# The last step of the last group: another order of its products, half sums in PSUM, an order written out, and two sums on GpSimd

## The chip, the cores and the metric

One Trainium2 chip, one core. The metric is the device time in microseconds of the whole program; it is one launch. TensorE (PE) multiplies, VectorE (DVE) and ScalarE (ACT) read and write PSUM and SBUF, GpSimd (POOL) works on SBUF only, SyncE (SP) issues the DMAs.

## The reference

Three stages follow each other, all in float32: an attention through 32 packed queries per head, a dense layer pair with SiLU, and a layer of 8 experts that are all computed for each token. Only the last stage matters here:

```python
P = ...                      # [2304, 8], normalised by rows and columns 8 times
out = zeros((2304, 512))
for e in range(8):
    h = maximum(x @ w1[e], 0)        # [2304, 1024]
    out += P[:, e:e+1] * (h @ w2[e]) # [2304, 512]
```

## The kernel before

The tokens of the last stage are three groups; groups 1 and 2 have 1024 tokens each. A group takes 16 steps, one for each expert `e` and half `fh` of its 1024 hidden columns; group 2, steps 32 to 47, ends the program. Matrices are held as a high part (ScalarE's cast) and a low part (VectorE's difference, `split`, L144 and L145), and a product is three matmuls, high by high, low by high, high by low.

In groups 1 and 2 each of the two products of a step is done by Strassen-Winograd's scheme with seven products of half-size blocks in place of eight; they are numbered 1 to 7. `up` computes h (transposed) into four blocks `hb`; `h_forms` makes from them the operands of the seven down products, each a high and a low tile out of pools with three buffers (`form`). `down7(s, p)` computes product `p` of step `s` for two halves `d` of the output rows: 6 matmuls into one PSUM bank of a pool `p3` of four, and the result is added to `M[p]`, one of seven sums that live through the group. Either the bank is first seeded with `M[p]` by ScalarE (L1125) and ScalarE copies the result back (L1137), or VectorE adds the bank to `M[p]` (L1141).

At the last step of a group the seven sums are combined: output blocks are M1 + M2, and M3, M5 and M4 after M6 (which has M1 added) and M7 have been added to them. In the kernel before, the last step of the last group (`LORD`) goes 1, 3, 5, 6, 7, 2, 4; M2 + M1 is one 1024-wide VectorE operation (L1143), M5 + M6 and M3 + M5 (L1145, L1146) stand behind product 6, M5 + M7 and M7 + M6 (L1149, L1151) behind product 7, and product 4 is folded with M7 by VectorE, one half at a time (L1133). `flush` sends the blocks out from the SP queue: 512 KB whole (L1107) or 256 KB by halves (L1109).

`moe_step(s)` makes the order of the text: per position `n` it draws the next form, computes `up` of step `s` and `down7` of step `s - 1`, and fetches weights three products ahead (`w2_get`, `w2_block`). At `s = 48` there is no `up` any more, only the down products of step 47. The parts of the program before step 17 of this stage run under `tc.manual_schedule` with PE, DVE and ACT: on these engines the instructions keep the order of the text. From step 17 on, the scheduler of the tile framework orders the instructions of each engine itself, by the text's order and by when it takes their inputs to be ready. Instructions inside a manual region keep their order among each other; those outside may go between them.

Of the kernel before, what the change touches and what calls it, by code (L numbers as in the profile page):

```python
# [9 lines left out]
F32 = mybir.dt.float32  # L10
# [14 lines left out]
NB = 512  # L25
# [79 lines left out]
def fused_kernel(  # L105
# [647 lines left out]
    G0 = 2 * NE  # L753
    ORD = [1, 2, 6, 7, 5, 3, 4]
    DORD = [1, 3, 7, 5, 6, 2, 4]
    LORD = [1, 3, 5, 6, 7, 2, 4]

    def dord(s):
        return LORD if s == NS - 1 else DORD

# [309 lines left out]
    def h_forms(s):  # L1070

        b11, b12, b21, b22 = (hb[s, f, t] for f in range(2) for t in range(2))

        def form(p, x):
            hi = st["hi"].tile([128, 2, NB], F32R, tag="hi", name=f"hi{s}_{p}")
            lo = st["lo"].tile([128, 2, NB], F32R, tag="lo", name=f"lo{s}_{p}")
            split(hi, lo, x)
            hf[s, p] = hi, lo

        form(1, b11)  # L1080
        yield
        form(3, b22)
        yield
        dve.tensor_tensor(b11, b12, b11, op=ALU.subtract)
        dve.tensor_tensor(b12, b22, b12, op=ALU.subtract)
        if dord(s) is DORD:
            form(7, b12)
            yield
        form(5, b11)
        yield  # L1090
        dve.tensor_tensor(b22, b22, b11, op=ALU.subtract)
        form(6, b22)
        yield
        if dord(s) is LORD:
            form(7, b12)
            yield
        form(2, b21)
        yield
        dve.tensor_tensor(b21, b21, b22, op=ALU.subtract)
        form(4, b21)  # L1100
        yield

    def flush(t, g, dh, th, d=None):
# [4 lines left out]
        else:  # L1108
            nc.sync.dma_start(o[:, d], t[:, d])  # L1109

    def down7(s, p):

        g, e, fh = steps[s]
        first, last = (e, fh) == (0, 0), (e, fh) == (NE - 1, 1)
        if first:
            M[p] = unit([128, 2, NB], F32, f"M{g}{p}")
        (hi, lo), w = hf.pop((s, p)), w2f.pop((s, p))
        for d in ((1, 0) if p == DORD[0] else (0, 1)):
            ps = p3.tile([128, 512], F32, tag="y", name=f"d{s}{p}{d}")
            m = M[p][:, d]  # L1120
            early = last and p == 2 and dord(s) is LORD
            fold = last and p in (6, 2, 4) and not early
            seed = not first and (fold or early or d == 0)
            if seed:
                act.copy(out=ps, in_=m)  # L1125
            n = 0
            for c in range(2):
                for l, r in ((0, hi), (0, lo), (1, hi)):
                    pe.matmul(ps, w[:, l, c, 128 * d:128 * d + 128], r[:, c],  # L1129
                              start=(n == 0 and not seed), stop=(n == 5), skip_group_check=seed)  # L1130
                    n += 1
            if fold:
                dve.tensor_tensor(m, ps, M[{6: 1, 2: 1, 4: 7}[p]][:, d], op=ALU.add)  # L1133
                if p != 6:
                    flush(M[p], g, p // 4, 0, d)
            elif seed or first:
                act.copy(out=m, in_=ps)  # L1137
                if early:
                    flush(M[p], g, 0, 0, d)
            else:  # L1140
                dve.tensor_tensor(m, ps, m, op=ALU.add)  # L1141
        if last and p == 3 and dord(s) is LORD:
            dve.tensor_tensor(M[2], M[2], M[1], op=ALU.add)  # L1143
        if last and p == 6:
            dve.tensor_tensor(M[5], M[5], M[6], op=ALU.add)  # L1145
            dve.tensor_tensor(M[3], M[3], M[5], op=ALU.add)  # L1146
            flush(M[3], g, 0, 1)
        if last and p == (7 if dord(s) is LORD else 6):
            dve.tensor_tensor(M[5], M[7], M[5], op=ALU.add)  # L1149
            flush(M[5], g, 1, 1)  # L1150
            dve.tensor_tensor(M[7], M[7], M[6], op=ALU.add)  # L1151

    X, Y, Z, cp = {}, {}, {}, {}

# [225 lines left out]
        cvn.drain()  # L1380


    def moe_step(s):
        swap = s + 1 < NS and steps[s + 1][0] != steps[s][0]
        hform = h_forms(s - 1) if s > G0 else iter(())
        next(hform, None)
        for n, p in enumerate(ORD):
            if s < NS:
                for i in range(2):
                    up(s, i, p)  # L1390
                if swap:
                    nc.sync.dma_start(x_tile(2, p).bitcast(F32), xfd[p])
                q = 7 * s + n + AHEAD
                if q < 7 * NS:
                    w1_get(q // 7, ORD[q % 7])
                q += 3
                if q < 7 * NS and ORD[q % 7] in (1, 2, 4):
                    w1_block(q // 7, ORD[q % 7])
            if s > G0:
                next(hform, None)  # L1400
                down7(s - 1, dord(s - 1)[n])
            if s == G0 and n == 0:
                load_w2(G0, 0, "r1")
                load_w2(G0, 1, "r1")
            q = 7 * (s - 1) + n + AHEAD
            if G0 <= q // 7 < 2 * G0:
                next(forms)
            elif 2 * G0 <= q // 7 < NS:
                w2_get(q // 7, dord(q // 7)[q % 7])
            q += 3  # L1410
            if 2 * G0 <= q // 7 < NS and dord(q // 7)[q % 7] in (1, 2, 4):
                w2_block(q // 7, dord(q // 7)[q % 7])
            if G0 < s < 2 * G0 - 1 and n == 3:
                next(xg2[0], None)
                next(xg2[0], None)
        if s == 2 * G0 - 2:
            for _ in xg2[0]:
                pass
        if s < NS and s % 2 == 0:
            load_pb(steps[s][0], steps[s][1] + 1)  # L1420

    with tc.manual_schedule(engines={mybir.EngineType.PE, mybir.EngineType.DVE, mybir.EngineType.Activation}):
        sk = sinkhorn()
        next(sk)
        for g in (1, 2):
            for k in range(4):
                tc.keep_in_program_order(nc.sync.dma_start(
                    x2d[k, :, TOK[g]:TOK[g] + 2 * NB],
                    x2[2 - g][k][:, TOK[g] % SB:TOK[g] % SB + 2 * NB]))
        for s_ in (a2a_st, x2a_st, x2b_st, gt_st, hp_st, pt_st, pg_st):  # L1430
            s_.close()
        for name, n in (("xf", 7), ("cp", 5), ("xr", 2), ("pb", 2)):
            open_(name, n, side="left", keep=True)
        open_("acc", 2 * LATE)
        st["u0"], u0_st = pool("pu", 2, space=PSUM, side="left", reuse_waits="tile")

        def chain(*gens):
            for g in gens:
                yield from g

        xg = x_forms(1, x_keep, (4, 4))
        comb = combine()
        for s in range(G0 + 1):
            for j in range(2):
                g, n, h, m = (w2s, s, w1s, s + 2) if j else (w1s, s + 1, w2s, s)
                if s < G0:
                    up0(s, j)
                    sum0(s, j)
                    adv(g, n, 2)
                    adv(g, n, 3)  # L1450
                    relu0(s, j)
                    if 2 * s + j >= 13:
                        next(xg, None)
                if s > 0:
                    down0(s - 1, j)
                if s < G0:
                    adv(g, n, 4)
                    adv(h, m, 1)
                    if s > 0:
                        next(sk, None)  # L1460
                    if s > 2 * LATE + 2:
                        next(comb, None)
                    if 2 * s + j >= 13:
                        next(xg, None)
                    if (s, j) == (G0 - 1, 0):
                        for _ in xg:
                            pass
            if s == G0 - 2:
                for p in ORD[:2]:
                    w1_block(G0, p, "S")  # L1470
            if s == G0 - 3:
                load_pb(1, 0)
            if s == G0 - 1:
                for p in ORD[:AHEAD]:
                    w1_get(G0, p)
        for name in ("acc", "r2", "gh", "xx", "po"):
            closers[name].close()
        u0_st.close()
        st["m"], s_ = pool("pm", 2, space=PSUM, side="left", reuse_waits="tile"); ctx.enter_context(s_)
        for name, n in (("hb", 6), ("hi", 3), ("lo", 3), ("rb", 2)):  # L1480
            open_(name, n, keep=True)
        forms = chain(*(w2_forms(s) for s in range(G0, 2 * G0)))
        xg2 = [x_forms(2, x_store, (1, 2))]
        moe_step(G0)
    for s in range(G0 + 1, NS + 1):
        moe_step(s)

# [51 lines left out]
```

## Time and profile before

| | us |
|---|---|
| median of 3 runs | 1782.55 (1781.41 to 1782.70) |
| the profiled execution | 1782.22 |
| its span, first to last instruction | 1780.5 |

The profile is of one execution. Times in its views are us from the span's start; "idle before" is the time in which the engine had nothing to do just before the first instruction of the row, with what ended it. PEld is TensorE's load of weights, which overlaps its matmuls. The granted clock of TensorE is given as a share of 2.4 GHz. TensorE is busy in 99% of the span, VectorE in 82%, ScalarE in 61%; the last step takes about the last 24 us.

### The profile page before, as it was taken

How to read it: one execution, taken by the hardware profiler on the slowest of the kernel's cores; microseconds unless marked ns; L12 is line 12 of the kernel's file. 1: busy time of each engine (PE TensorE's matmuls, PEld its weight loads, DVE VectorE, ACT ScalarE, POOL GpSimd, SP SyncE). 2: the span in 40 equal slices, each digit the busy share in tenths (PEclk: the TensorE clock that was granted, in tenths of full speed). 3: DMA queues.
4: the chain of work that ended last, by engine and by line, in shares of the span. 5: the costliest groups of instructions: out<-in, count | busy, mean ns of one | idle time of the engine just before them, and what ended most of it. 6: DMA issues, size and time to landing. Idle time of an engine off the chain costs nothing.

```text
span 1780.5 us, 24855 instructions
## 1 busy us (share of the span) xinstructions
PE 1765.2 (99%) x9324; PEld 1495.3 (84%) x9324; DVE 1453.2 (82%) x1950; ACT 1084.5 (61%) x1728; POOL 1.0 (0%) x8
## 2 busy tenths in 40 slices
PE   7999999999999999999999999999999999999998
PEld 5899999988888888888888888888888888888887
DVE  7968796758996989999889999887777777777778
ACT  6866776656664666666666666656555555555555
POOL 0000000000000000000000000000000000000000
PEclk9999999999999999999999999999999999999999
DMA  9326676965664755456545556855555444545442
GB/s 350 143 96 213 241 263 247 335 224 180 213 233 156 256 186 183 162 201 209 169 171 177 172 188 202 317 203 170 157 170 165 155 156 146 172 155 172 148 130 95
DMA packets 141496, 341.72 MB, mean 192 GB/s; under 512 B 11952, under 2 KB 49472, under 8 KB 140480
## 3 DMA queue, kind: packets, MB, share of 16 engines
q1 hardware_dynamic: 141376, 340.14, 56.2%
q8 instruction: 73, 1.20, 0.3%
q14 instruction: 47, 0.39, 0.1%
HBM read 256.66 MB, written 83.44 MB: 191 GB/s over the span
## 4 chain that ended last, share of the span: by engine, by line
PE 95%; DVE 3%; ACT 1%; issue 0%; DMA 0%; DVEq 0%; SPq 0%; ACTq 0%
PE d L1129 34%; PE X L1177 20%; PE Z L1177 10%; PE g2w L689 8%; PE g L600 5%; PE d L1036 5%; PE Y L1177 5%; PE u L1004 3%; PE g L654 3%; PE u L1007 2%; PE u L193 1%; PE s L193 0%; DMA kq<-in_kT_dram 0%; PE lg L1211 0%; DVE nmx L270 0%
## 5 line engine op out<-in xcount | busy, mean ns | idle before, releaser
L145 DVE TENSOR_TENSOR lo<-hb,hi 128x1024 fp32r<-128x1024 f32 x224 | 273.7, 1222 | 33.0 <-ACT hi L144 32.0
L1129 PE MATMUL d<-hi,w2f 128*128 128x512 f32 x896 | 294.2, 389 | 0.0
L1177 PE MATMUL X<-xf,w1l 128*128 128x512 f32 x1152 | 276.9, 389 | 0.0
L144 ACT CAST hi<-hb 128x1024 fp32r<-128x1024 f32 x224 | 235.3, 1051 | 66.8 <-PE d L1129 61.6
L1177 PEld LDWEIGHTS X<-xf,w1l 128*128 128x128 f32 x1152 | 216.2, 188 | 44.9
L1137 ACT COPY M<-d 128x512 f32<-128x512 f32 x234 | 137.2, 588 | 141.5 <-PE d L1129 140.6
L1141 DVE TENSOR_TENSOR M<-d,M 128x512 f32<-128x512 f32 x204 | 140.4, 688 | 100.2 <-PE d L1129 100.2
L1129 PEld LDWEIGHTS d<-hi,w2f 128*128 128x128 f32 x896 | 168.2, 188 | 35.1
L1129 PE MATMUL d<-lo,w2f 128*128 128x512 f32 x448 | 174.3, 389 | 0.0
L1129 PE MATMUL d<-hi,w2l 128*128 128x512 f32 x512 | 167.8, 389 | 0.0
L689 PE MATMUL g2w<-ring,woh 128*128 128x384 f32 x576 | 147.6, 337 | 0.0
L1125 ACT COPY d<-M 128x512 f32<-128x512 f32 x216 | 127.1, 589 | 22.1 <-DVE M L1141 20.4
L1129 PE MATMUL d<-hi,w2g 128*128 128x512 f32 x384 | 125.7, 389 | 0.0
L1129 PEld LDWEIGHTS d<-hi,w2l 128*128 128x128 f32 x512 | 96.1, 188 | 20.2 <-ACT d L1125 0.4
L689 PEld LDWEIGHTS g2w<-ring,woh 128*128 128x128 f32 x576 | 102.9, 188 | 8.6 <-issue 7.5
L1184 ACT COPY cp<-X 128x512 f32<-128x512 f32 x128 | 74.3, 581 | 47.2 <-PE X L1177 47.0
L1129 PE MATMUL d<-lo,w2l 128*128 128x512 f32 x256 | 99.6, 389 | 0.0
L1129 PEld LDWEIGHTS d<-lo,w2f 128*128 128x128 f32 x448 | 84.1, 188 | 17.4
L1177 PE MATMUL Y<-xf,w1f 128*128 128x512 f32 x384 | 97.4, 389 | 0.0
L689 PE MATMUL g2w<-ring,wol 128*128 128x384 f32 x288 | 96.3, 334 | 0.0
L144 ACT CAST w1f<-rb 128x512 fp32r<-128x512 f32 x96 | 59.8, 624 | 57.2 <-PE d L1129 43.4
L1177 PE MATMUL Z<-xf,w1f 128*128 128x512 f32 x384 | 92.2, 389 | 0.0
(220 smaller groups left out, 3428.7 us busy)
## 6 DMA issues: line engine op xcount, KB each, us to landing
r<-in_moe_w_dram SPq DMA_DIRECT2D x128, 512.0 KB, 4.1
w1l<-w1d SPq DMA_DIRECT2D x128, 512.0 KB, 4.0
w1d<-po SPq DMA_DIRECT2D x64, 512.0 KB, 4.4
w2d<-w2f SPq DMA_DIRECT2D x64, 512.0 KB, 4.2
w2l<-w2d SPq DMA_DIRECT2D x64, 512.0 KB, 3.5
rb<-in_moe_w_dram SPq DMA_DIRECT2D x96, 256.0 KB, 2.6
sb<-in_moe_w_dram SPq DMA_DIRECT2D x48, 256.0 KB, 2.7
pb<-pd SPq DMA_DIRECT2D x16, 512.0 KB, 5.2
```

The lines of the kernel that those rows point to most:

```text
L144: act.copy(out=hi, in_=raw)
L145: eng.tensor_tensor(out=lo, in0=raw, in1=hi.bitcast(F32), op=ALU.subtract)
L600: pe.matmul(ps, lhs[:, fs], rhs, start=(n == 0), stop=(n == 5))
L654: pe.matmul(ps[:, :HS], lhs, rhs, start=(n == 0), stop=(n == 3 * nf - 1))
L689: pe.matmul(ps[:, :TW], lhs[:, f % 2, ds], ring[f // 2][:, 2 * (f % 2) + rhs, q], start=(n == 0 and not on), stop=(n == 11), skip_group_ch ...
L1036: pe.matmul(ps, h[:, l, f % 2, 128 * tt:128 * tt + 128], w[:, f % 2], start=(fh == 0 and n == 0), stop=(fh == 1 and n == 11))
L1125: act.copy(out=ps, in_=m)
L1129: pe.matmul(ps, w[:, l, c, 128 * d:128 * d + 128], r[:, c], start=(n == 0 and not seed), stop=(n == 5), skip_group_check=seed)
L1137: act.copy(out=m, in_=ps)
L1141: dve.tensor_tensor(m, ps, m, op=ALU.add)
L1177: pe.matmul(ps, w[:, l, c, 128 * i:128 * i + 128], x[:, r, c], start=(n == 0 and p in (1, 7)), stop=(n == 5), skip_group_check=p in (2, 6, ...
L1184: act.copy(out=t, in_=ps)
```

## The change

The last step of the last group goes through its products as 1, 3, 5, 6, 2, 7, 4. Form 2 is made before form 7, and both are drawn before product 6; form 4 is drawn before product 2. From position 2 on (form 6 and product 5) PE, DVE and ACT run in the order of the text. After the first half of products 5, 6, 2 and 7, both banks of the next product are allocated and, where they are seeded, written (`start7`). Product 7 is seeded in both halves and evicted by ScalarE; M6 (with M1 in it) is added to M7 by halves right after product 6's halves, so that product 7's banks start from M7 + M6. M2 + M1 and M3 + M5 go to GpSimd. M3 + M6 stands ahead of product 7, M5 + M7 behind it. The last step of group 1 keeps its operations.

```diff
-    LORD = [1, 3, 5, 6, 7, 2, 4]
+    LORD = [1, 3, 5, 6, 2, 7, 4]
...
         form(6, b22)
         yield
+        form(2, b21)
+        yield
         if dord(s) is LORD:
             form(7, b12)
             yield
-        form(2, b21)
-        yield
         dve.tensor_tensor(b21, b21, b22, op=ALU.subtract)
         form(4, b21)
         yield
...
+    def start7(s, p, d):
+        first, last = steps[s][1:] == (0, 0), steps[s][1:] == (NE - 1, 1)
+        end = last and dord(s) is LORD
+        if first and p not in M:
+            M[p] = unit([128, 2, NB], F32, f"M{steps[s][0]}{p}")
+        ps = p3.tile([128, 512], F32, tag="y", name=f"d{s}{p}{d}")
+        seed = not first and (d == 0 or (last and p in (6, 2, 4)) or (end and p == 7))
+        if seed:
+            act.copy(out=ps, in_=M[p][:, d])
+        open7[p, d] = ps, seed
...
+        def total(a, b, d=slice(0, 2), eng=dve):
+            eng.tensor_tensor(M[a][:, d], M[a][:, d], M[b][:, d], op=ALU.add)
+        if end and p == 7:
+            total(3, 6)
+            flush(M[3], g, 0, 1)
+        for n, d in enumerate((1, 0) if p == DORD[0] else (0, 1)):
+            if (p, d) not in open7:
+                start7(s, p, d)
+            ps, seed = open7.pop((p, d))
             m = M[p][:, d]
...
-            if fold:
+            if last and (p in (6, 4) or (p == 2 and not end)):
                 dve.tensor_tensor(m, ps, M[{6: 1, 2: 1, 4: 7}[p]][:, d], op=ALU.add)
                 if p != 6:
                     flush(M[p], g, p // 4, 0, d)
+                elif end:
+                    total(7, 6, d)
             elif seed or first:
                 act.copy(out=m, in_=ps)
-                if early:
+                if end and p == 2:
                     flush(M[p], g, 0, 0, d)
             else:
                 dve.tensor_tensor(m, ps, m, op=ALU.add)
-        if last and p == 3 and dord(s) is LORD:
-            dve.tensor_tensor(M[2], M[2], M[1], op=ALU.add)
...
+            if end and n == 0 and p in LORD[2:6]:
+                for x in range(2):
+                    start7(s, LORD[LORD.index(p) + 1], x)
+        if end and p == 3:
+            total(2, 1, eng=nc.gpsimd)
+        if end and p == 5:
+            total(3, 5, eng=nc.gpsimd)
+        if end and p == 7:
+            total(5, 7)
+            flush(M[5], g, 1, 1)
...
+            if s == NS and n == 2:
+                tail.enter_context(tc.manual_schedule(engines=FIXED))
...
                 next(hform, None)
+                if s == NS and n == 3:
+                    next(hform, None)
                 down7(s - 1, dord(s - 1)[n])
```

## Rows read from the trace of the kernel before

**Rows 1.** Page: busy us of each engine, share of the span, instructions.
```profile
PE 1765.2 (99%) x9324; PEld 1495.3 (84%) x9324; DVE 1453.2 (82%) x1950; ACT 1084.5 (61%) x1728; POOL 1.0 (0%) x8
```

**Rows 2.** Chain that ended last, from 1735 us: start, us, what.
```profile
1750.93 2.72 PE Z L1177 x12
1753.65 11.14 PE d L1129 x48
...
1764.81 1.06 ACT hi L144
...
1774.63 1.24 DVE M L1151
```

**Rows 3.** Timeline, PE and PEld, last step: start, us, engine line op [idle before].
```profile
1758.92 0.39 PE L1129 MATMUL d<-hi,w2l 128*128 128x512 f32 x1
...
1761.74 0.19 PEld L1129 LDWEIGHTS d<-hi,w2l 128*128 128x128 f32 x1 [0.36 <-ACT d L1125]
...
1773.51 0.19 PEld L1129 LDWEIGHTS d<-lo,w2g 128*128 128x128 f32 x1 [0.55 <-DVE lo L145]
...
1775.68 0.39 PE L1129 MATMUL d<-hi,w2g 128*128 128x512 f32 x1
```

**Rows 4.** Timeline, VectorE, last step.
```profile
1760.94 1.22 DVE L145 TENSOR_TENSOR lo<-hb,hi 128x1024 fp32r<-128x1024 f32 x1
1762.08 0.68 DVE L1141 TENSOR_TENSOR M<-d,M 128x512 f32<-128x512 f32 x1
1762.68 0.68 DVE L145 TENSOR_TENSOR w2g<-sb,w2g 128x512 fp32r<-128x512 f32 x1
1763.28 1.22 DVE L145 TENSOR_TENSOR lo<-hb,hi 128x1024 fp32r<-128x1024 f32 x1
1764.81 0.69 DVE L1141 TENSOR_TENSOR M<-d,M 128x512 f32<-128x512 f32 x1 [0.31 <-PE d L1129]
1765.90 1.22 DVE L145 TENSOR_TENSOR lo<-hb,hi 128x1024 fp32r<-128x1024 f32 x1 [0.40 <-ACT hi L144]
...
1768.24 1.22 DVE L1099 TENSOR_TENSOR hb<-hb,hb 128x1024 f32<-128x1024 f32 x1
...
1773.38 1.22 DVE L1149 TENSOR_TENSOR M<-M,M 128x1024 f32<-128x1024 f32 x1
1774.63 1.23 DVE L1151 TENSOR_TENSOR M<-M,M 128x1024 f32<-128x1024 f32 x1
1775.99 1.29 DVE L1133 TENSOR_TENSOR M<-d,M 128x512 f32<-128x512 f32 x2
```

**Rows 5.** Timeline, ScalarE, last step.
```profile
1759.66 1.05 ACT L144 CAST hi<-hb 128x1024 fp32r<-128x1024 f32 x1
1760.61 0.58 ACT L1137 COPY M<-d 128x512 f32<-128x512 f32 x1
1761.09 0.60 ACT L1125 COPY d<-M 128x512 f32<-128x512 f32 x1
1761.84 1.05 ACT L144 CAST hi<-hb 128x1024 fp32r<-128x1024 f32 x1 [0.15 <-PE d L1129]
```

**Rows 6.** SP queue's timeline, and one window: us, engines' busy time, clock, DMA share, GB/s.
```profile
1774.62 0.38 SPq L1107 DMA_DIRECT2D out_dram<-M  x1
1776.71 0.93 SPq L1109 DMA_DIRECT2D out_dram<-M  x2
...
1774.00:1775.00 1.00, 1.00 (x6) 0.79 (x5) 0.97 (x2) 0.00 (x0) 0.00 (x0) 1.00 1.05 391
```

**Rows 7.** GpSimd's groups by line: shapes, count | busy us, mean ns | idle before.
```profile
masks.py:199 POOL TENSOR_SCALAR_AFFINE_SELECT ident<-ident 128x128 f32<-128x128 f32 x1 | 0.3, 292 | 0.0
L153 POOL MEMSET ones<- 128x128 f32 x1 | 0.2, 205 | 0.0
```

**Rows 8.** Windows at the end and the start; clock is third from the end.
```profile
1776.07:1780.50 4.43, 0.00 (x1) 0.00 (x0) 1.21 (x2) 0.00 (x0) 0.00 (x0) 1.00 0.59 219
2.00:4.00 2.00, 0.00 (x0) 0.00 (x0) 0.41 (x1) 0.01 (x1) 0.00 (x0) 1.00 0.92 349
...
5.14 1.18 PE L193 MATMUL s<-kq,pTs 64*32 64x288 f32 x8 [5.14 <-DMA kq<-in_kT_dram]
```

More of the change, by code (lines that the diff above doesn't have):

```diff
@@ L1109, in flush @@
             nc.sync.dma_start(o[:, d], t[:, d])
+    open7 = {}
+    def start7(s, p, d):
[8 more added lines that the diff above has]
+        open7[p, d] = ps, seed
     def down7(s, p):
@@ L1114, in down7 @@
         first, last = (e, fh) == (0, 0), (e, fh) == (NE - 1, 1)
+        end = last and dord(s) is LORD
         if first:
-            M[p] = unit([128, 2, NB], F32, f"M{g}{p}")
+            M.pop(p, None)
         (hi, lo), w = hf.pop((s, p)), w2f.pop((s, p))
-        for d in ((1, 0) if p == DORD[0] else (0, 1)):
-            ps = p3.tile([128, 512], F32, tag="y", name=f"d{s}{p}{d}")
-            m = M[p][:, d]
[L1121 to L1126, printed above, removed]
+        def total(a, b, d=slice(0, 2), eng=dve):
[7 more added lines that the diff above has]
+            ps, seed = open7.pop((p, d))
+            m = M[p][:, d]
+            k = 0
             for c in range(2):
@@ L1129, in down7 @@
                     pe.matmul(ps, w[:, l, c, 128 * d:128 * d + 128], r[:, c],
-                              start=(n == 0 and not seed), stop=(n == 5), skip_group_check=seed)
-                    n += 1
-            if fold:
+                              start=(k == 0 and not seed), stop=(k == 5), skip_group_check=seed)
+                    k += 1
+            if last and (p in (6, 4) or (p == 2 and not end)):
                 dve.tensor_tensor(m, ps, M[{6: 1, 2: 1, 4: 7}[p]][:, d], op=ALU.add)
@@ L1141, in down7 @@
                 dve.tensor_tensor(m, ps, m, op=ALU.add)
-        if last and p == 3 and dord(s) is LORD:
-            dve.tensor_tensor(M[2], M[2], M[1], op=ALU.add)
-        if last and p == 6:
-            dve.tensor_tensor(M[5], M[5], M[6], op=ALU.add)
-            dve.tensor_tensor(M[3], M[3], M[5], op=ALU.add)
+            if end and n == 0 and p in LORD[2:6]:
[8 more added lines that the diff above has]
+            flush(M[5], g, 1, 1)
+        if last and not end and p == 6:
+            total(5, 6)
+            total(3, 5)
             flush(M[3], g, 0, 1)
-        if last and p == (7 if dord(s) is LORD else 6):
-            dve.tensor_tensor(M[5], M[7], M[5], op=ALU.add)
+            total(5, 7)
             flush(M[5], g, 1, 1)
-            dve.tensor_tensor(M[7], M[7], M[6], op=ALU.add)
+            total(7, 6)
     X, Y, Z, cp = {}, {}, {}, {}
@@ L1380, in fused_kernel @@
         cvn.drain()
+    FIXED = {mybir.EngineType.PE, mybir.EngineType.DVE, mybir.EngineType.Activation}
+    tail = ExitStack()
     def moe_step(s):
@@ L1420, in moe_step @@
             load_pb(steps[s][0], steps[s][1] + 1)
-    with tc.manual_schedule(engines={mybir.EngineType.PE, mybir.EngineType.DVE, mybir.EngineType.Activation}):
+    with tc.manual_schedule(engines=FIXED):
         sk = sinkhorn()
@@ L1486, in fused_kernel @@
         moe_step(s)
+    tail.close()
 _INS = ['qT', 'kT', 'v', 'pT', 'moe_w_in', 'moe_w_out', 'moe2_w_gate', 'moe2_w1', 'moe2_w2']
```

## The prediction

> **What bounds the kernel now.** I read the busy times first: TensorE is busy 99% of the span and no other engine is close [rows 1], so the body of the kernel is paced by matmuls, and the change leaves the number of matmuls alone. It can move only the last step. So I went to the chain of waits over the last 46 us [rows 2]. It runs through TensorE until 1764.79 us; there it passes to ScalarE's form of product 2 and stays on VectorE to the end. In the last 16 us it is VectorE's queue that decides. TensorE's own timeline [rows 3] shows what is to be won: a wait of 0.36 us before product 5 (for a seed) and one of 0.55 us before product 4 (for its low part). The last matmul ends at 1775.68 + 0.39 = 1776.07, and the last fold of VectorE at 1775.99 + 1.29 = 1777.28 [rows 4], because its queue was behind: 0.7 us of it is the fold itself, some 0.5 us is backlog. So about 0.9 + 0.5 = 1.4 us is all that the change can win by order. Behind the fold stand two output transfers and the end of the program: 1780.5 - 1777.28 = 3.2 us.
>
> **Durations.** Back to back, VectorE's 1024-wide operation costs 1.14 us (1760.94 to 1762.08) and its 512-wide one 0.60 (1762.08 to 1762.68); one that reads what the operation just before it wrote or must not overwrite too early starts only after that one's full length, 0.03 to 0.13 us later (1773.38 + 1.22, then 1774.63; 1774.63 + 1.23, then 1775.99) [rows 4], so a dependent 512-wide pair costs 0.60 + 0.71. ScalarE's 1024-wide cast costs 0.95 and a 512-wide copy 0.48 back to back, 1.05 and 0.6 until the result is there [rows 5]. Twelve matmuls, one product, cost 2.72 us [rows 2], half a product 1.36; its result is there 0.17 later (0.39 for a matmul that issues every 0.227).
>
> **The last step in the written order.** From product 5 on, VectorE and ScalarE keep the order of the text.
> - Before it little moves. The seed of product 5 is queued on ScalarE behind form 6 and an eviction, as now (1761.09 + 0.60) [rows 5], so product 5 again starts at 1761.8; its halves are done at 1763.4 and 1764.7.
> - ScalarE: now the cast of form 7 runs at 1761.84 [rows 5], while product 5 is computed, and VectorE's low part of form 7 at 1763.28 [rows 4], in time that VectorE had free. In the new text both stand behind product 5's evictions. ScalarE waits for 1763.4, evicts, writes the two seeds of product 6 (to 1764.9; they cover product 6's start at 1764.5), then casts form 2 (to 1765.9) and form 7 (to 1766.8).
> - VectorE has nothing to do from 1762.6 until product 5's second half, evicts it at 1764.8, waits for the cast, and then has this queue: low part 2 from 1765.9 and low part 7, 1.14 each, to 1768.2; for each half of product 6 the fold with M1 and the sum into M7, 2 x (0.60 + 0.71), to 1770.8; the low part of product 4's weight, 0.60, which has run by 1763.3 now and moves into this stretch, to 1771.4; and only then the difference for form 4 (L1099), 1.22, to 1772.6.
> - ScalarE casts form 4 at 1772.7 to 1773.7. Queued behind this cast are the eviction of product 2 (0.48) and the seeds of product 7 (0.6 for the first): 1774.7. TensorE finished product 2 at about 1770.3 and waits for this seed until 1774.8, some 4.4 us.
> - Products 7 and 4 are then 24 matmuls, 5.44 us, and nothing of the rest is later than they (product 4's seeds are written while product 7's second half runs, its low part is done at 1773.8 to 1775): last result at 1780.4, fold 0.68, end 1781.1 where it is 1777.28 now. **The order costs +3.9 us.** The wait of 0.55 us before product 4 and the backlog at the end go, and are in this sum; the wait for product 7's seed is what is late next.
> - The output transfers: product 2's two and M3's are out early, hidden by products 7 and 4. M5's 512 KB is issued when product 7's eviction and the sum are done, about 1779.7, half a microsecond before the first half of product 4 instead of two (1774.62 and 1776.71) [rows 6]. At 391 GB/s, what the row of a full window shows [rows 6], 1 MiB takes 2.7 us from about 1780.7, where the last half alone would end at 1782.9: between 0 and 0.7 us; I take 0.5, since three transfers overlap as they do in the row.
> - Product 7's weight is fetched one product later and product 2's block one earlier; three products or more, 2.72 us each [rows 2], lie between the fetch and the use: nothing, and if that cover were gone, a wait of TensorE at product 2 or 7.
>
> **The two sums on GpSimd.** They take 2 x 1.14 us from VectorE, and the queue above is already without them. What one costs on GpSimd no row shows; ends: 1.22 us, VectorE's own length [rows 4], and 4.7 us, two operands one after the other at the rate of the 128-wide selection, 0.292 us [rows 7], times 8. I take 2.34 us, one pass at that row's rate, since it is the only row of GpSimd that reads and writes SBUF. At that length both sums are done before they are needed (1762.1 for product 2's seed at 1766.7, under 1770 for M3), even at 4.7. What they cost VectorE, whose adds read the same memory at the same time, is not shown either. One end is 0. The other is that a VectorE operation with both operands in SBUF waits as long as GpSimd's runs: the first sum (1759.8 to 1762.1) then pushes low part 6 and the eviction of product 3's second half, whose PSUM bank product 5's second half needs, by 0.9 us; the second, in the stretch where VectorE has no idle time, pushes the queue to form 4 by 1.8: 2.7 together (0.8 at 1.22 us a sum, 7.4 at 4.7). Nothing in the rows is nearer to one end, so I take half, 1.35 us.
> The Trainium skill (SBUF — State Buffer, "Who interferes with whom") says that a VectorE instruction with two SBUF inputs and a GpSimd instruction that reads SBUF exclude each other for the whole instruction; no row here has the two side by side. By it the 2.7 would hold in full, and the sum would be 1789.6. For the length, the skill (GPSIMD Engine Reference, 3.1) gives 4497 ns for 2048 columns, by which I estimate 2.2 us; the sum by it would be 0.1 us lower.
>
> **The sum.** 3.9 + 0.5 + 1.35 = +5.75 on a span of 1780.5: 1786.2. Outside the span the profiled execution has 1782.22 - 1780.5 = 1.72, and it lies 0.33 under the median 1782.55: 1786.2 + 1.72 + 0.33 = **1788.3 us**.
>
> **Rivals.**
> - GpSimd costs VectorE nothing: 1788.3 - 1.35 = 1786.9, with the transfers free as well 1786.4. For it: VectorE's adds keep their lengths whatever DMA and ScalarE do beside them. Against it: GpSimd does nothing after the first microsecond [rows 7], so these rows have no such meeting.
> - TensorE's clock falls while it waits for product 7. The last 24 matmuls then run at the lower of its two levels, 5.4 us more if all of them do, half of that if it rises again midway: 1791.0. Against it: the granted clock stands at 1.00 in the last 4.43 us, with no matmul in them, and at the start, where the first matmul comes at 5.14 us [rows 8]. For it: a 4.4 to 6 us wait between two loads occurs nowhere in the body. The Trainium skill (TensorE: Matmul & The Clock Gate, "What's actually happening") states that the clock drops to 1.2 GHz after an idle stretch; by that this rival would hold.
> - Not slower: the queue isn't late, because form 7 still slips into VectorE's idle time before 1764.8 and form 4's difference ends before about 1767.8 (product 2's end without waits, 1769.8, less a cast, an eviction and a seed). Then TensorE never waits, both waits of rows 3 and the backlog are gone: 1782.55 - 1.4 = 1781.2. It decides by whether the scheduler still moves these operations, that is whether the written order binds. For it: in the kernel before, the scheduler did such moves (forms 5 to 7 run ahead of their text). Against it: the whole region is put under the same kind of fixed order that the earlier parts have.
>
> **How the numbers follow.** Forecast (1787.3 to 1789.7) 0.50; GpSimd free 0.20; clock 0.15; not slower 0.15, where the change would also not do what it says. A difference below 0.2% (3.6 us, to 1786.1) can't be told from none. Half of the "free" case falls under that, and most of the last, with 0.03 for a gain above it, which would need more than twice the 1.4 us that are there: faster 0.03, same 0.22, slower 0.75. The range of 8 in 10 runs from 1784.0, which leaves out most of the last case, to 1791.8, which takes in the full 2.7 and the clock midway.
>
> **What would show it.** Right: TensorE idle for 4 to 6 us before the first matmul of product 7, waiting for ScalarE's seed; the difference for form 4 ending at 1772.6 or later on VectorE; both low parts 2 and 7 behind product 5's second eviction; VectorE adds of more than 1.3 us while GpSimd runs, if they collide. Wrong: low part 7 before 1764, no wait of TensorE over 1 us, or GpSimd's sums beside adds of 1.22 us.

## The result, and the profile after

The changed kernel takes 1791.51 us (median of six runs, 1790.06 to 1794.05) where the kernel before takes 1782.62 (1781.41 to 1782.77): 8.9 us more, ratio 1.0051 [1.004, 1.0061]. The forecast was 1788.3, slower, with a range from 1784.0 to 1791.8: the median lies 0.3 us inside the upper end, and three of the six executions lie above it. The profiled execution took 1791.83, its span is 1790.1, 9.6 over the span before. Where the kernel before ran again beside the experiments below, five of its executions took more than 2200 us, and its medians there leave them out. In this kernel the products' matmuls are line 1148, seeds 1122, ScalarE's evictions 1158, VectorE's 1162, folds 1152, the sums (`total`) 1135, the difference for form 4 still 1099.

The page's busy times, which answer to [rows 1]:

```profile
PE 1767.3 (99%) x9324; PEld 1495.8 (84%) x9324; DVE 1453.7 (81%) x1948; ACT 1085.5 (61%) x1730; POOL 6.7 (0%) x10
```

The number of matmuls is the same, TensorE's time is 2.1 us longer, and GpSimd has two instructions and 5.7 us more. The chain of waits over the last step (start, us, what), beside [rows 2]:

```profile
1767.13 4.56 DVE lo L145 x2
...
1774.95 1.15 DVE hb L1099
...
1777.71 0.50 ACT d L1122
...
1778.25 7.47 PE d L1148 x24
...
1785.75 0.69 DVE M L1152
```

The end is again decided by VectorE's queue, but now it goes through form 4's difference, ScalarE's seed (L1122) and 24 matmuls behind that. TensorE's timeline (start, us, instruction, idle before and its releaser), beside [rows 3]:

```profile
1764.82 0.51 PE L1148 MATMUL d<-hi,w2l 128*128 128x512 f32 x1 [0.58 <-DVE M L1162]
...
1771.54 0.39 PE L1148 MATMUL d<-hi,w2g 128*128 128x512 f32 x1
1778.25 0.80 PE L1148 MATMUL d<-hi,w2l 128*128 128x512 f32 x1 [6.32 <-ACT d L1122]
1778.84 0.63 PE L1148 MATMUL d<-lo,w2l 128*128 128x512 f32 x1
```

TensorE stands still for 6.32 us between product 2 and product 7, and the first matmuls of product 7 come 0.43 us apart (1778.84, the next at 1779.27) in place of 0.227. VectorE's timeline, beside [rows 4]:

```profile
1759.25 1.21 DVE L145 TENSOR_TENSOR lo<-hb,hi 128x1024 fp32r<-128x1024 f32 x1
1761.58 2.58 DVE L145 TENSOR_TENSOR lo<-hb,hi 128x1024 fp32r<-128x1024 f32 x1 [1.12 <-ACT hi L144]
1764.09 0.68 DVE L1162 TENSOR_TENSOR M<-d,M 128x512 f32<-128x512 f32 x1
1766.53 0.69 DVE L1162 TENSOR_TENSOR M<-d,M 128x512 f32<-128x512 f32 x1 [1.76 <-PE d L1148]
1767.13 4.56 DVE L145 TENSOR_TENSOR lo<-hb,hi 128x1024 fp32r<-128x1024 f32 x2
...
1774.27 0.68 DVE L145 TENSOR_TENSOR w2g<-sb,w2g 128x512 fp32r<-128x512 f32 x1
1774.87 1.22 DVE L1099 TENSOR_TENSOR hb<-hb,hb 128x1024 f32<-128x1024 f32 x1
...
1785.75 0.69 DVE L1152 TENSOR_TENSOR M<-d,M 128x512 f32<-128x512 f32 x1 [0.30 <-PE d L1148]
```

GpSimd's timeline, beside [rows 7]:

```profile
1760.69 2.40 POOL L1135 TENSOR_TENSOR M<-M,M 128x1024 f32<-128x1024 f32 x1 [1759.14 <-ACT M L1158]
1767.35 3.26 POOL L1135 TENSOR_TENSOR M<-M,M 128x1024 f32<-128x1024 f32 x1 [4.27 <-ACT hi L144]
```

The queue stands in the order that the forecast wrote out: low part 5 (1759.25), low part 6 (1761.58), product 3's and product 5's second evictions, low parts 2 and 7 (1767.13, together), product 6's folds and sums, the weight, the difference. The low parts (L145) from 6 on, 1.22 us each before, last 2.58 and, two together, 4.56; this standing still beside a sum of GpSimd is called the hold below. The first ends 1.07 us after GpSimd's first sum (1760.69 + 2.40 = 1763.09, 1761.58 + 2.58 = 1764.16). The pair is 2.2 us longer than two adds (2.36 in a run below), and its end lies 1.08 behind the end of GpSimd's second sum (1770.61, 1771.69). GpSimd's second sum itself took 0.86 longer than its first: it began while low part 2 was running. Of the pair it is low part 7 that is long, 3.43 us by itself. ScalarE, beside [rows 5]:

```profile
1776.18 1.04 ACT L144 CAST hi<-hb 128x1024 fp32r<-128x1024 f32 x1 [6.76 <-DVE hb L1099]
1777.13 0.58 ACT L1158 COPY M<-d 128x512 f32<-128x512 f32 x1
1777.60 1.11 ACT L1122 COPY d<-M 128x512 f32<-128x512 f32 x2
```

Form 4's cast, product 2's eviction and product 7's seeds, in that order: ScalarE waits 6.76 us for VectorE with an eviction and two seeds queued behind the cast. Windows (us, busy time of the five engines, granted clock, DMA share, GB/s), beside [rows 8]:

```profile
1769.00:1771.70 2.70, 2.70 (x13) 2.08 (x12) 2.70 (x2) 0.41 (x1) 1.62 (x1) 1.00 0.00 0
1771.70:1778.20 6.50, 0.23 (x2) 0.00 (x0) 5.26 (x7) 2.02 (x4) 0.00 (x0) 0.76 0.00 0
1778.20:1780.00 1.80, 1.75 (x4) 1.46 (x5) 1.41 (x2) 1.03 (x2) 0.00 (x0) 0.50 0.39 146
1780.00:1782.00 2.00, 2.00 (x6) 1.52 (x6) 0.00 (x0) 0.73 (x2) 0.00 (x0) 0.53 0.98 362
1782.00:1784.00 2.00, 2.00 (x11) 1.60 (x10) 0.38 (x1) 1.46 (x3) 0.00 (x0) 1.00 0.09 32
```

The granted clock is 1.00 until product 2 ends, falls during the wait, is 0.50 (the lower level, 1.2 GHz) when product 7 begins, and is back at 1.00 by 1782. Last, the SP queue, beside [rows 6]:

```profile
1779.64 5.61 SPq L1107 DMA_DIRECT2D out_dram<-M  x2
1785.48 1.33 SPq L1109 DMA_DIRECT2D out_dram<-M  x2
```

From the last fold's end (1785.75 + 0.69) to the span's end is 3.66 us, 3.22 before: M5's 512 KB (the second L1107, issued at 1784.9) and product 4's two halves go out together, as forecast (nothing moves from 1784 to 1785.5, 373 to 393 GB/s from 1786 to 1788.5).

### The profile page after: what moved, and what is told of

Read it like the earlier page. It is cut to its first block, busy times and chain, and to the rows that moved or that the text cites. A ratio compares the mean times of both kernels' runs of the same rounds, so it can differ in the third digit from the quotient of the medians.

```text
span 1790.1 us, 24865 instructions
## 1 busy us (share of the span) xinstructions
PE 1767.3 (99%) x9324; PEld 1495.8 (84%) x9324; DVE 1453.7 (81%) x1948; ACT 1085.5 (61%) x1730; POOL 6.7 (0%) x10
## 4 chain that ended last, share of the span: by engine, by line
PE 94%; DVE 4%; ACT 1%; issue 1%; DMA 1%; SPq 0%; ACTq 0%; DVEq 0%
PE d L1148 33%; PE X L1205 19%; PE Z L1205 10%; PE g2w L689 8%; PE g L600 5%; PE d L1036 5%; PE Y L1205 5%; PE u L1004 3%; PE g L654 3%; PE u L1007 2%; PE u L193 1%; DVE lo L145 1%; PE s L193 0%; DMA xf<-xfd 0%; DMA kq<-in_kT_dram 0%
## 5 line engine op out<-in xcount | busy, mean ns | idle before, releaser
L145 DVE TENSOR_TENSOR lo<-hb,hi 128x1024 fp32r<-128x1024 f32 x224 | 277.0, 1237 | 34.8 <-ACT hi L144 33.9
L1122 ACT COPY d<-M 128x512 f32<-128x512 f32 x217 | 127.4, 589 | 20.4 <-DVE M L1162 20.0
L1205 PE MATMUL Z<-xf,w1l 128*128 128x512 f32 x384 | 92.2, 389 | 0.0
```

The source lines that it names most:

```text
L145: eng.tensor_tensor(out=lo, in0=raw, in1=hi.bitcast(F32), op=ALU.subtract)
L1122: act.copy(out=ps, in_=M[p][:, d])
L1205: pe.matmul(ps, w[:, l, c, 128 * i:128 * i + 128], x[:, r, c], start=(n == 0 and p in (1, 7)), stop=(n == 5), skip_group_check=p in (2, 6, ...
```

## The experiments

Three theories: the fixed order is the cost (form 4's difference stands behind product 6's work on VectorE, and its cast ahead of product 7's seeds on ScalarE); GpSimd's sums hold VectorE's adds; the clock is lost in the wait. The kernel before ran beside each group: 1781.91 (e1, e2, e3, e4), 1781.90 (a0, e3b, e5, e8) and 1782.46 (e7, e9, e10, e11).

**e1: both sums back on VectorE, all else as changed.**

```diff
-            total(2, 1, eng=nc.gpsimd)
+            total(2, 1)
...
-            total(3, 5, eng=nc.gpsimd)
+            total(3, 5)
```

> The changed kernel with its two GpSimd sums (M2 + M1, M3 + M5) back on VectorE. My theory of the 8.9 us: 3.9 for the written order and 0.5 for the output queue, 2.7 because a VectorE operation with both operands in SBUF stands still while GpSimd's sum runs, 2.0 because the matmuls of product 7 start at the lower clock after the wait. By it the 2.7 go, and M3 + M5 puts 1.1 into VectorE's queue before form 4: TensorE's wait for product 7 is about 5.5 us, which may or may not lower the clock: 1788.1 to 1790.1 us. All of VectorE's low parts take 1.22 us again. Rival, GpSimd costs VectorE nothing: the sums only add to VectorE's queue, 1791.5 + 1.1 = 1792.6 us.

1790.21 us (1788.79 to 1790.54), ratio 1.0045 [1.0029, 1.0061], 0.1 above the expected range. Low parts 2 and 7 in its VectorE timeline, and product 7's start in its TensorE timeline:

```profile
1767.27 2.35 DVE L145 TENSOR_TENSOR lo<-hb,hi 128x1024 fp32r<-128x1024 f32 x2
```

```profile
1776.18 0.79 PE L1148 MATMUL d<-hi,w2l 128*128 128x512 f32 x1 [4.83 <-ACT d L1122]
```

All low parts take 1.22 again, so the long adds are GpSimd's doing. The wait before product 7 is still 4.83 us and the clock still falls (0.50 in 1776 to 1778), so most of the loss isn't GpSimd's.

**e2: neither sum**; the output lacks them.

```diff
-        if end and p == 3:
-            total(2, 1, eng=nc.gpsimd)
-        if end and p == 5:
-            total(3, 5, eng=nc.gpsimd)
```

> The changed kernel with the two GpSimd sums left out altogether (M2 lacks M1 and M3 lacks M5 in the output). It measures the written order alone. My theory: 1782.6 + 3.9 + 0.5 = 1787.0 us if the clock stays up through a wait of about 4.4 us, up to 1789.0 if it falls; form 4's difference ends 3.9 us after product 3's... that is, TensorE waits 4 to 4.8 us before product 7. Rival, the sums on GpSimd cost nothing: 1791.5 us as with them.

1789.85 us (1789.47 to 1790.43), ratio 1.0045 [1.0029, 1.0061]; expected were 1789.0 at most. Its VectorE timeline:

```profile
1758.57 1.22 DVE L145 TENSOR_TENSOR lo<-hb,hi 128x1024 fp32r<-128x1024 f32 x1
1760.90 1.23 DVE L145 TENSOR_TENSOR lo<-hb,hi 128x1024 fp32r<-128x1024 f32 x1 [1.11 <-ACT hi L144]
...
1766.24 2.36 DVE L145 TENSOR_TENSOR lo<-hb,hi 128x1024 fp32r<-128x1024 f32 x2 [0.59 <-ACT hi L144]
...
1771.77 1.22 DVE L1099 TENSOR_TENSOR hb<-hb,hb 128x1024 f32<-128x1024 f32 x1
```

and its TensorE timeline:

```profile
1775.16 0.79 PE L1148 MATMUL d<-hi,w2l 128*128 128x512 f32 x1 [4.43 <-ACT d L1122]
```

This is the forecast's order term by itself: low part 6 stands where it did before (1760.90; 1760.94 in [rows 4]), the difference ends at 1772.99 (forecast 1772.6) and product 7 starts at 1775.16 (forecast 1774.8; 0.16 of the difference is that low part 5 starts at 1758.57 here and at 1758.41 in the kernel before). Counted from low part 5's start (1759.25 in the changed kernel, 1758.57 here) product 7 starts 19.00 us later there and 16.59 here: the two sums on GpSimd cost 2.41 (on VectorE, in e1, where it is 1776.18 - 1758.94 = 17.24, they cost 0.65). Of the 2.41 the first sum's hold leaves 0.21 (low part 2 starts 7.88 after low part 5, and 7.67 here, where it waits 0.59 for its cast), the second 2.20 (4.56 against 2.36). The time falls by less than 2.41, since here the clock stays low for longer: from product 7's start to the last fold's end it is 8.93 us (1775.16 to 1784.09), 8.19 in the changed kernel.

**e3 and e3b: TensorE kept busy while it waits for product 7**, with matmuls whose result nobody reads.

```diff
+                if s == NS and n == 5:
+                    fill = st["m"].tile([128, 512], F32, tag="x", name="fill")
+                    for _ in range(42):      # e3b: range(24)
+                        pe.matmul(fill[:, :128], ident, ident, start=True, stop=True)
                 down7(s - 1, dord(s - 1)[n])
```

> The changed kernel with 42 small matmuls of the identity by itself into a spare PSUM bank between product 2 and product 7, so that TensorE is busy in most of its 6.3 us wait. My theory (the clock falls in the wait, and ten matmuls of product 7 run at 0.43 us in place of 0.23): granted clock 1.00 throughout, product 7's matmuls 0.23 us apart, 2.0 us less: 1789.5 us. Rival, the first matmuls of product 7 are slow for another reason (banks or tiles that other engines use): still 0.43 us apart and 1791.5 us.

1791.91 us (1791.74 to 1792.14), ratio 1.0057 [1.0039, 1.0075]. The filling was too long: it ran from 1770.37 to 1779.9, some 3 us past the point at which the seed was there, so the time says nothing of what the clock costs. The clock was 1.00 and product 7's matmuls stood 0.23 apart. The shorter filling was run beside the changed kernel again:

> The changed kernel as it is, once more, so that the runs beside it are compared on one chip: 1791 to 1792 us, some 9 us above the kernel before.

> The changed kernel with 24 small matmuls in TensorE's wait for product 7 in place of 42 (each of the 42 took 0.23 us, so that all of them outlasted the wait by 2.9 us and hid what the clock gave back). 24 take 5.5 us and end within the wait of 6.3. My theory: product 7 starts when it does in the changed kernel, at clock 1.00, its matmuls 0.23 us apart: 2.0 us below the changed kernel. Rival, the filling matmuls cost elsewhere what they give: no gain.

The changed kernel: 1791.54 (1791.33 to 1791.78), ratio 1.0054 [1.004, 1.0067]. With the filling: 1789.70 (1788.72 to 1791.85), 1.0045 [1.0031, 1.0059], 1.84 less; one of its four executions is as slow as the changed kernel, and the two intervals overlap, so the gain rests on the rows. TensorE's timeline of e3b:

```profile
1769.89 5.52 PE L1439 MATMUL fill<-ident 128*128 128x128 f32 x48
1776.36 0.50 PE L1148 MATMUL d<-hi,w2l 128*128 128x512 f32 x1 [0.94 <-ACT d L1122]
1776.69 0.39 PE L1148 MATMUL d<-lo,w2l 128*128 128x512 f32 x1
1776.92 0.63 PE L1148 MATMUL d<-hi,w2l 128*128 128x512 f32 x2
```

its last fold, and product 7's start in the changed kernel run again:

```profile
1782.32 0.69 DVE L1152 TENSOR_TENSOR M<-d,M 128x512 f32<-128x512 f32 x1 [0.26 <-PE d L1148]
```

```profile
1777.15 0.80 PE L1148 MATMUL d<-hi,w2l 128*128 128x512 f32 x1 [6.31 <-ACT d L1122]
```

Product 7 starts no earlier after low part 5 (1757.38) than in the changed kernel, 18.98 us against 19.00, and runs at the full clock. From its start to the last fold's end (1783.01) is 6.65 us, where the changed kernel has 8.19 and, run again, 8.81 (1777.15 to 1785.96): the clock costs 1.5 to 2.2 us. In e3b's profiled execution the span ends 5.39 us after the last fold, so the comparison of spans shows less of it than the medians.

**e4: the last step without the written order**, GpSimd and half sums kept; and **e9: the same with the sums on VectorE** (e1's edit too).

```diff
-            if s == NS and n == 2:
-                tail.enter_context(tc.manual_schedule(engines=FIXED))
```

> The changed kernel without the fixed order on TensorE, VectorE and ScalarE in the last step; the order of products, the half sums and the GpSimd sums stay. My theory (the written order holds the queue up): the scheduler moves form 7's low part and the weight of product 4 ahead again, TensorE waits under 2.5 us in all before products 7 and 4, the clock stays at 1.00; GpSimd still stops VectorE for 1 to 3 us: 1782.5 to 1786 us. Rival, the new order of the products and the sums in PSUM halves are what costs: 1788 us or more.

> The changed kernel without the fixed order and with both sums on VectorE: what is left of the change is the product order and the half sums. My theory: no VectorE operation over 1.3 us, TensorE's wait before product 7 under 1.5 us in place of 2.2, 1 to 2.5 us below the same with GpSimd (1785.5), that is 1783 to 1784.5. Rival, GpSimd doesn't matter here: 1785.5 or more, since VectorE gets 2.3 us of work back.

e4: 1785.53 us (1784.41 to 1787.39, nine runs), 1.0021 [1.0011, 1.0031]. e9: 1784.04 (1782.48 to 1787.57, eleven), 1.001 [1.0001, 1.0019]. VectorE's timeline of e4:

```profile
1763.99 1.21 DVE L145 TENSOR_TENSOR lo<-hb,hi 128x1024 fp32r<-128x1024 f32 x1
...
1766.42 1.22 DVE L1099 TENSOR_TENSOR hb<-hb,hb 128x1024 f32<-128x1024 f32 x1
1767.55 3.43 DVE L145 TENSOR_TENSOR lo<-hb,hi 128x1024 fp32r<-128x1024 f32 x1
```

TensorE's timeline of e4, and below it the first matmul of product 7 in e9:

```profile
1768.56 0.39 PE L1148 MATMUL d<-lo,w2g 128*128 128x512 f32 x1
...
1773.45 0.50 PE L1148 MATMUL d<-hi,w2l 128*128 128x512 f32 x1 [2.24 <-ACT d L1122]
```

```profile
1772.57 0.50 PE L1148 MATMUL d<-hi,w2l 128*128 128x512 f32 x1 [1.27 <-ACT d L1122]
```

Left to the scheduler, a low part runs in VectorE's idle time ahead of product 5's second eviction, and form 4's difference at 1766.42, before 1767.8, as the third rival wanted. The low part that runs early is that of form 2, not of form 7: product 2's matmuls with it come at 1768.56, while the long one at 1767.55 ends only at 1770.98. TensorE's wait before product 7 is 2.24 us in e4 (low part 7, ahead of product 6's folds, is held to 3.43 by GpSimd) and 1.27 in e9, and the clock is 1.00 through products 7 and 4. So the written order is the largest term. GpSimd costs 1.5 us here by the medians and 2.0 by the ratios, whose intervals overlap; by the rows, product 7 starts 15.15 us after low part 5 in e4 and 13.08 in e9, 2.07.

**e5: one line of the order changed: form 4 is drawn after product 2's matmuls, not before.**

```diff
-                next(hform, None)
+                if s < NS or n != 4:
+                    next(hform, None)
```

> The changed kernel with one line moved: form 4 is drawn after product 2 in place of before it, so that ScalarE's eviction of product 2 and the seeds of product 7 no longer stand behind form 4's cast. GpSimd's sums stay. My theory (the cast that waits for VectorE holds the seeds back): product 7's first seed is written as soon as M7 is summed, TensorE waits about 2 us before product 7 and about 2 us before product 4, no wait is long enough for the clock to fall: 4.5 us below the changed kernel, 1787.0 us. Rival, VectorE's late queue alone sets the end, wherever the cast stands on ScalarE: within 1 us of the changed kernel.

1787.07 us (1786.96 to 1788.87), ratio 1.0031 [1.0018, 1.0043]; the forecast for this run was 1787.0. TensorE's timeline:

```profile
1772.69 0.50 PE L1148 MATMUL d<-hi,w2l 128*128 128x512 f32 x1 [1.76 <-ACT d L1122]
...
1777.19 0.50 PE L1148 MATMUL d<-hi,w2g 128*128 128x512 f32 x1 [1.46 <-ACT d L1122]
```

Product 7's seeds no longer stand behind form 4's cast: one wait of 6.3 becomes two of 1.76 and 1.46, the clock stays at 1.00, and 4.5 us come back with the GpSimd sums still in place.

**e8: the kernel before with one sum (M2 + M1) on GpSimd.**

```diff
-            dve.tensor_tensor(M[2], M[2], M[1], op=ALU.add)
+            nc.gpsimd.tensor_tensor(M[2], M[2], M[1], op=ALU.add)
```

> The kernel before with one operation moved: M2 + M1 on GpSimd. My theory (a VectorE operation with both operands in SBUF stands still while GpSimd's sum runs): the sum takes 2.4 us, low part 6 beside it ends about 1.2 us later than before, which pushes VectorE's queue and product 5: 0.5 to 1.5 us slower. Rival, GpSimd relieves VectorE of 1.14 us: 0 to 0.5 us faster.

1782.31 us (1781.26 to 1783.15), ratio 1.0002 [0.9993, 1.001]: no difference to be measured. GpSimd's timeline and VectorE's:

```profile
1760.18 2.64 POOL L1143 TENSOR_TENSOR M<-M,M 128x1024 f32<-128x1024 f32 x1 [1758.63 <-ACT M L1137]
```

```profile
1761.08 2.82 DVE L145 TENSOR_TENSOR lo<-hb,hi 128x1024 fp32r<-128x1024 f32 x1 [0.52 <-ACT hi L144]
```

The hold is there (low part 6 takes 2.82, GpSimd's sum 2.64), but the scheduler put product 4's low part of the weight where the sum had stood, and VectorE's queue ends at 1777.61 where it ended at 1777.28. The expected loss of 0.5 to 1.5 us didn't come: here the order can move, and the hold falls into slack. That isn't so wherever the order is free, as e4 shows.

**e7: a written order made from these findings**: form 2 between product 5's seeds and its evictions, form 4's difference ahead of form 7, product 4's weight two positions earlier, ahead of product 5, both sums on VectorE; and **e10: e7 with M2 + M1 on GpSimd.**

```diff
         form(2, b21)
         yield
+        dve.tensor_tensor(b21, b21, b22, op=ALU.subtract)
         if dord(s) is LORD:
             form(7, b12)
             yield
-        dve.tensor_tensor(b21, b21, b22, op=ALU.subtract)
         form(4, b21)
...
         if end and p == 7:
+            total(3, 5)
             total(3, 6)
...
-            total(2, 1, eng=nc.gpsimd)
-        if end and p == 5:
-            total(3, 5, eng=nc.gpsimd)
+            total(2, 1)                  # e10: eng=nc.gpsimd kept
...
-                if s == NS and n == 3:
+                if s == NS and n == 2:
+                    start7(s - 1, 5, 0)
                     next(hform, None)
...
-            elif 2 * G0 <= q // 7 < NS:
+            elif 2 * G0 <= q // 7 < NS and q != 7 * NS - 1:
                 w2_get(q // 7, dord(q // 7)[q % 7])
+                if q == 7 * NS - 3:
+                    w2_get(NS - 1, 4)
```

> A version that keeps the change's product order, its half sums and a fixed order of the last step, but another order, and VectorE for both sums: form 2 is drawn between product 5's seed and its eviction, form 4's difference between product 5's eviction and form 7, product 4's weight is split before product 5, M3 + M5 stands just ahead of M3 + M6. Worked out from the rows of before: form 4's low part ends at about 1771.5, TensorE waits only for product 5's seed (0.3 us), the last fold ends at about 1776.3 where it ended at 1777.28, and the output queue gives 0.2 to 0.5 back: 0.4 to 0.9 us below the kernel before, which the rounds may not tell from none. Rival, halves, seeds and product order of the change cost something by themselves: 1 us or more above the kernel before.

> The new order with one operation moved, M2 + M1 on GpSimd. My theory: the sum of 2.4 us starts before form 6's low part and holds it for about 1.4 us, product 3's eviction behind it follows late, and the second half of product 5, which needs that bank, waits about 0.9 us; the rest of the order has slack on VectorE of less than that: 0.3 to 1.2 us slower than the new order without it. Rival, GpSimd relieves VectorE: 0 to 0.5 us faster.

e7: 1781.68 us (1781.22 to 1782.37, eleven runs), ratio 0.9995 [0.9986, 1.0005], 9.8 below the changed kernel and not to be told from the kernel before. Its VectorE timeline:

```profile
1765.10 1.22 DVE L1096 TENSOR_TENSOR hb<-hb,hb 128x1024 f32<-128x1024 f32 x1
...
1775.81 0.69 DVE L1153 TENSOR_TENSOR M<-d,M 128x512 f32<-128x512 f32 x1 [0.25 <-PE d L1149]
```

Form 4's difference (here L1096) runs at 1765.10, 9.8 us earlier than in the changed kernel. The last fold ends at 1776.50, 0.78 earlier than before, and half a microsecond of this is given back behind it: 3.7 us to the span's end where it was 3.22. e10: 1783.63 (1782.51 to 1785.13, eleven), 1.0009 [1.0, 1.0017]; 1.95 over e7 by the medians, 0.9 by the spans (1781.1 and 1780.2); 0.3 to 1.2 were expected. Its VectorE timeline:

```profile
1760.13 2.88 DVE L145 TENSOR_TENSOR lo<-hb,hi 128x1024 fp32r<-128x1024 f32 x1 [0.47 <-ACT hi L144]
1762.93 0.68 DVE L1163 TENSOR_TENSOR M<-d,M 128x512 f32<-128x512 f32 x1
```

and its TensorE timeline:

```profile
1763.66 0.50 PE L1149 MATMUL d<-hi,w2l 128*128 128x512 f32 x1 [0.87 <-DVE M L1163]
```

The held low part delays product 3's eviction, and TensorE waits 0.87 us for that bank. This explains the spans' 0.9. Each span is of one execution, and e10's was a quick one (1782.90, 0.73 under its median; e7's 1782.02, 0.34 over its own), so no row shows the rest of the 1.95.

**e11: e1 with half of M3 + M5 on GpSimd while VectorE evicts from PSUM** (a single execution).

```diff
+            if end and n == 0 and p == 5:
+                total(3, 5, 0, eng=nc.gpsimd)
...
-            total(3, 5)
+            total(3, 5, 1)
```

> The changed kernel with its sums on VectorE, except the first half of M3 + M5, which goes to GpSimd as soon as ScalarE has evicted that half: it then runs while VectorE evicts product 5's second half, an operation with one operand in PSUM and one in SBUF. If only operations with two operands in SBUF are held up, that eviction takes 0.69 us as everywhere. Rival, GpSimd holds up any VectorE operation: 1 us or more, or it starts only when GpSimd is done.

1788.93 us. GpSimd's timeline:

```profile
1763.67 1.29 POOL L1135 TENSOR_TENSOR M<-M,M 128x512 f32<-128x512 f32 x1 [1762.12 <-ACT M L1158]
```

and VectorE's:

```profile
1764.33 0.69 DVE L1162 TENSOR_TENSOR M<-d,M 128x512 f32<-128x512 f32 x1 [2.08 <-PE d L1148]
```

The eviction has one operand in PSUM and one in SBUF; all but its last 0.06 us ran beside GpSimd's sum (to 1764.96), and it kept its 0.69 us. What is held is the add with both operands in SBUF.

## Why the prediction was right, and what it mis-sized

The direction and the mechanism of the order held; the forecast was 3.2 us low, because one term was put at nothing (the clock, 1.54) and one was taken too small (GpSimd's hold, 1.06). The way from [rows 4]'s last fold at 1777.28 to the changed kernel's at 1786.44, term by term:

| step | forecast | measured | from |
|---|---|---|---|
| difference, cast, eviction, seed: start of product 7 without the sums | 1774.8 | 1775.16 | e2 |
| the two sums on GpSimd | 1.35 | 2.41 | changed kernel against e2 |
| body of the profiled execution later | none | 0.68 | low part 5, same pair |
| product 7's start to the last fold, full clock | 6.3 | 6.65 | e3b |
| clock in products 7 and 4 | none | 1.54 | 8.19 - 6.65 |
| output queue behind the last fold | 0.5 | 0.44 | 3.66 - 3.22 |

1775.16 + 2.41 + 0.68 + 6.65 + 1.54 = 1786.44. The terms come from three profiles and are defined so that they must add up; how firm each is shows in the runs that repeat it (the clock costs 1.5 to 2.2 in two profiles of the changed kernel). The misses, 0.36 + 1.06 + 0.68 + 0.35 + 1.54 - 0.06, make 3.9 on the span. The forecast's 2.05 from the span to the median measured 1.41, since this profile lies 0.32 above its median and the one before lay 0.33 below: that leaves 3.3, the 3.2 up to rounding.

- **The order term was right.** Place and cause are as forecast: low parts 2 and 7 behind product 5's second eviction, form 4's difference after product 6's sums and the weight's low part, its cast ahead of the seeds. e2 shows it alone, 0.36 us off; e5 and e7 show that it is this order, not halves or product order, that costs. The other 0.35 is in the 24 matmuls and their end. (1781.1 less 1777.28 is 3.8, not the 3.9 of the sum.)
- **The GpSimd term was mis-sized.** I bounded it by 0 and 2.7 and took half, 1.35; it measured 2.41, nearly the upper end. The step that failed is "nothing in the rows is nearer to one end, so I take half". The sum's length was right (2.40 against 2.34), and the hold is whole: the add ends 1.07 to 1.09 us after GpSimd, about an add's 1.14. The two parts were 0.21 and 2.20 where I had 0.9 and 1.8 at full hold. The first hold does delay product 5's second eviction by the 0.9 (7.28 us after low part 5, 6.39 in e2), but that falls mostly into a wait for ScalarE's cast that VectorE had anyway. By the Trainium skill (SBUF — State Buffer, "Who interferes with whom") a VectorE add with two SBUF inputs and GpSimd's reads exclude each other for a whole instruction, and whichever is issued first goes first; the 2.58 and 4.56 agree, and so do GpSimd's own 0.86 and the free eviction of e11.
- **The clock was the largest miss: the rival came true beside the forecast, not in its place.** The sum has nothing for it. I gave it 0.15 on [rows 8], in which the clock stands at 1.00 with no matmul; those stretches are behind the last matmul and before the first, and the wait here was between the two. After the waits of 4.43 to 6.32 us in these runs (e1, e2, e11, the changed kernel twice) matmuls began at 0.50; after those of 0.9 to 2.24 (e3b, e4, e5, e9) at 1.00. Length alone does not decide it: 4.43 us without a matmul left the clock at 1.00 at the end of the kernel before [rows 8], and 4.43 lowered it in e2. The 5.4 us for all 24 matmuls was an upper end: 8 to 13 ran slowly, for 1.5 to 2.6 us (e1: 1776.18 to 1785.40 is 9.22, less 6.65).
- **That the time fell inside the range was partly luck.** The upper end, 1791.8, is said to take in the full 2.7 and the clock midway, but 1788.3 + 1.35 + 2.7 is 1792.35. Both came true, and the time stays under 1791.8 since each cost less than that: 2.41 and 1.54.
- **"GpSimd costs nothing" fell** with e1 and e2, **"not slower"** with the changed kernel's own timeline: the written order binds on VectorE, and low part 7 runs after 1768 (1771.69 - 3.43). e4 shows what that rival would have needed.

What stays open: what makes up the rest of e10's 1.95 over e7, of which the rows show 0.9; what, besides the length of a wait, decides whether the clock falls in it; and why the clock was low for 8 matmuls in one profile of the changed kernel and for 11 in the next.

## What to carry to other kernels

When a scheduler's order is replaced by a written one, write out each engine's queue with times and look for what the next product needs: an operation with slack (a cast for the last product) put ahead of one without (a seed for the next) costs its whole wait. A sum moved from VectorE to GpSimd is no gift where VectorE's adds have both operands in SBUF: here two sums of 1.14 us delayed product 7 by 0.65 us on VectorE and by 2.41 on GpSimd. TensorE's waits of 4.43 us and more in this step had a second price, matmuls at half the clock behind them; where such a wait can't be removed, splitting it (e5) or filling it (e3b) kept the clock here.

## What the runs showed of the hardware that was not expected

- GpSimd's sum of two fp32 tiles in SBUF takes 2.40 us for 1024 columns and 1.29 for 512, about twice VectorE's 1.22 and 0.69; an add of VectorE with two SBUF operands that meets it ends 1.07 to 1.09 us behind it (an add is 1.14 back to back), and its row only looks longer (2.58 us, the hold isn't shown as a wait); one with a PSUM operand kept its length (e11).
- It works both ways: a GpSimd sum issued while VectorE was in such an add took 2.64 to 2.69 (e4, e8, e10) or 3.26.
- Product 7's matmuls of 512 columns stand 0.427 us apart at a granted clock of 0.50 and 0.227 at 1.00, so the pace does not quite halve. A filling matmul of 128 columns counts as two records and takes 0.23 us.
